# Row maxima in PSUM, a second staging tile, token subtractions on VectorE, and an order list that counts what it measured: a fused attention and two feed-forward layers

## The chip, the cores and the metric

The kernel runs on one core of a Trainium2 chip. Its engines are TensorE (PE, with its weight loads as PEld), VectorE (DVE), ScalarE (ACT), GpSimd (POOL) and SyncE (SP, which here only issues DMA transfers). The metric is the device time of one execution in microseconds. Lower is better.

## The reference

```python
scores = scale * np.matmul(q, k.transpose(0, 1, 3, 2))      # q, k, v: [4, 8, 576, 64]
log_f = np.log(np.clip(f, 0.0001, 1.0))
cum = np.cumsum(log_f, axis=-1)
decay = cum[:, :, :, None] - cum[:, :, None, :]
scores = np.where(causal, -1000000000.0, scores + decay)
scores = scores - np.max(scores, axis=-1, keepdims=True)
attn = np.exp(scores)
attn = attn / (np.sum(attn, axis=-1, keepdims=True) + 1e-09)
attn_out = np.matmul(attn, v)
...
x = attn_out.transpose(0, 2, 1, 3).reshape(2304, 512)
h = x @ w_in                                                # 512 -> 2048
x = (h * (1.0 / (1.0 + np.exp(-1.702 * h)))) @ w_out        # 2048 -> 512
g = x @ w_gate                                              # 512 -> 1536
out = (g * (1.0 / (1.0 + np.exp(-g))) * (x @ w_val)) @ w_out2
```

The weights arrive as 64-bit floats, the rest as 32-bit floats.

## The kernel before, in words

Attention handles the 32 heads in 16 pairs P. For each pair `maxima` multiplies queries with keys once (L338, and L341 for the decay), takes the maximum of each query's row on DVE (L345, with a mask that makes later keys very small), and transposes the maxima (L379). `products` multiplies again in split precision (L403), now with the maxima as a further operand, so that ACT can take the exponential straight from PSUM (L408); POOL cuts the causal edge (L412). PE then forms the values (L433) and the sums of the rows (L463). The sums travel through small transfers to a reciprocal on DVE (L478, L479) and back, and L486 divides. L338, L341 and L403 run as pairs on the upper and lower half of the array's rows, L433 as pairs on halves of its columns, L463 on quarters; the rest use the whole array.

The two layers work on token groups of 768, in two halves of 384 columns, with seven products in place of eight for each block of 2x2. `xbuild` loads a group's tokens and forms the four differences that this needs (L636, on POOL); ACT rounds them (L649) and DVE takes the remainder (L650), into the tile X. `chain` runs seven blocks of six matmuls (L673 to L675) for one unit of 256 hidden columns; ACT copies (L693) or DVE adds (L696) the blocks out of their PSUM banks. `gate`, `value` and `rounded` form the activation and split it (L757); `second` multiplies with the output weights (L777 to L779) and accumulates on DVE (L789).

`prepare` turns one unit's weights from 64 bits to 32: two loads into the tile stg, one ACT row (L556), four DVE rows (L557, L559, L561, L563), then four combinations (L579) or a split (L572), all in the tile pre, and stores to DRAM. There are 34 units; eight of them fall into attention. `stream` brings them back, rounded by L605 and L606.

What stands where on each engine is a list: each piece of work is given to `add` with its engine, a planned duration, a rank, what it reads and writes, and the PSUM banks that it takes and gives back. `order` plays the list through, each engine taking the piece of lowest rank that is ready, and so writes out one fixed order per engine. On the chip each engine works strictly through its row; semaphores hold it back where data are missing. The planned times set the order alone.

Of the kernel before, what the change touches and what calls it, by code (L numbers as in the profile page):

```python
# [31 lines left out]
LAT_PE, LAT = 330, 110  # L32
# [6 lines left out]
PSTEP, PLAG, XLEAD, PSTART = 15000, 5, 40, 205000  # L39
# [4 lines left out]
class Program:  # L44
# [12 lines left out]
    def add(self, eng, dur, rank, emit, reads=(), writes=(), lat=None, after=0, take=(), give=(), size=0):  # L57
# [16 lines left out]
        if lat is None:  # L74
            lat = LAT_PE if eng == "pe" else LAT
        self.ops.append((eng, dur, rank, emit, sorted(deps), lat, after, tuple(take), tuple(give), size))

    def order(self):
# [15 lines left out]
        moved = 0  # L94

        def at(n):
            k = len(ops[n][7])
            if not k:
                return ready_at[n]
            if len(spare) < k or held.get(ops[n][7][0][0], 0) + k > CAP:  # L100
                return 1e12
            return max(ready_at[n], spare[k - 1][0])

        while any(pools.values()):
            best = None
            for eng, pool in pools.items():
# [3 lines left out]
                n = min((n for n in pool if at(n) <= now), key=lambda n: (ops[n][2], n))  # L110
# [5 lines left out]
            o = ops[n]  # L116
            free[eng] = now + o[1]
            lat = o[5]
# [13 lines left out]
            out.append((now, n))  # L132
# [13 lines left out]
def kernel(  # L146
# [86 lines left out]
    junk = ap_.tile([128, 512], BF16, name="junk")  # L233
# [88 lines left out]
    def maxima(P):  # L322
# [21 lines left out]
        def rmax(c, t, e, o, n, end, floor=NEG):  # L344
            nc.vector.tensor_tensor_reduce(  # L345
                out=junk[:, 0:n], in0=bk("mx", P, c, e)[:, o:o + n], in1=maskw[:, end - n:end], scale=1.0,
                scalar=floor, op0=ALU.add, op1=ALU.max, accum_out=mt[i2][:, t, 32 + 64 * e:33 + 64 * e])

        def first(c, dur, *parts):
            add("pe", dur, P + RANK["max"], lambda: rmm(c, *parts), KM, take=[("mx", P, c, e) for e in range(2)])  # L350
# [5 lines left out]
        for e in range(2):  # L356
            add("dve", 720, P + RANK["maxv"], lambda e=e: rmax(0, 3, e, 0, 512, 512), MW, [("mt", i2, 3, e)], give=[("mx", P, 0, e)])
        first(1, 2 * cols(128) + 2 * cols(384), (0, 0, 0, 128), (128, 2, 0, 384))
        for e in range(2):
            add("dve", 600, P + RANK["maxv"], lambda e=e: rmax(1, 2, e, 128, 384, 512), MW + [("mx", P, 1, e)], [("mt", i2, 2, e)])  # L360
            add("dve", 320, P + RANK["maxv"], lambda e=e: rmax(1, 0, e, 0, 128, 512), MW + [("mt", i2, 2, e)], [("mt", i2, 0, e)],
                give=[("mx", P, 1, e)])
        first(2, 4 * cols(256), (0, 1, 0, 256), (256, 4, 0, 256))
        for e in range(2):
            add("dve", 400, P + RANK["maxv"], lambda e=e: nc.vector.tensor_reduce(
# [584 lines left out]
```

## Time and profile before

| | us |
|---|---|
| median of 3 runs | 1039.8 |
| lowest, highest run | 1036.37, 1040.24 |
| the profiled execution's own time | 1040.38 |
| its span, from the first to the last instruction | 1038.7 |
| PE busy | 996.5 (96%) |
| DVE busy | 788.2 (76%) |
| ACT busy | 554.2 (53%) |
| POOL busy | 219.6 (21%) |

The span is one execution. PE's busy time is that of rows whose ends are modelled, so it includes slow matmuls; what a busy PE achieves is read from how many matmuls start in a stretch.

### The profile page before, as it was taken

What the parts mean: (1) busy time and instruction counts of PE and PEld (TensorE: products, weight loads), DVE (VectorE), ACT (ScalarE), POOL (GpSimd) and SP (SyncE); (2) the same over time, 40 slices, a digit from 0 to 9 for tenths busy, and PEclk for the clock granted to TensorE, in tenths of its full rate; (3) what the DMA queues carried; (4) which work ended last, traced back from release to release, by engine and by line L of the source; (5) the groups of instructions that cost most, each with busy time, mean ns of one, the idle gap of its engine ahead of it and who ended that gap; (6) DMA issues with size and microseconds to landing.
All of it is one profiled execution on the core that took longest, in us unless ns stands there. A gap on an engine that the chain in (4) does not pass through costs nothing.

```text
span 1038.7 us, 18067 instructions
## 1 busy us (share of the span) xinstructions
PE 996.5 (96%) x6665; PEld 936.3 (90%) x6665; DVE 788.2 (76%) x1361; ACT 554.2 (53%) x947; POOL 219.6 (21%) x311
## 2 busy tenths in 40 slices
PE   6999989998899999999999899999899999999998
PEld 4766666778899999989999899999899999999998
DVE  7788779966798888988788897978855559555454
ACT  4656546665666566555654564453563556444420
POOL 3656559610422202122012200201000201000000
PEclk9999999999999999999999999999899999999999
DMA  4567778467878978978879867957655443555212
GB/s 167 188 203 225 222 261 253 140 205 230 282 232 270 322 261 303 309 287 284 297 245 315 283 227 248 325 184 269 207 166 175 157 142 115 160 163 148 95 61 102
DMA packets 118792, 226.63 MB, mean 218 GB/s; under 512 B 15120, under 2 KB 70416, under 8 KB 118704
## 3 DMA queue, kind: packets, MB, share of 16 engines
q1 hardware_dynamic: 118704, 225.48, 66.1%
q8 instruction: 52, 0.85, 0.3%
q14 instruction: 36, 0.29, 0.1%
HBM read 173.23 MB, written 52.13 MB: 217 GB/s over the span
## 4 chain that ended last, share of the span: by engine, by line
PE 79%; DVE 11%; DMA 5%; issue 2%; ACT 2%; SPq 1%; DVEq 0%; ACTq 0%
PE bank L673 10%; PE bank L674 9%; PE bank L675 9%; PE bank L778 8%; PE bank L777 8%; PE bank L779 8%; PE xx L673 3%; PE bank L403 3%; PE xx L674 3%; PE xx L675 3%; PE xx L433 3%; PE xx L778 2%; PE xx L779 2%; PE xx L777 2%; DVE junk L345 2%
## 5 line engine op out<-in xcount | busy, mean ns | idle before, releaser
L778 PE MATMUL bank<-arena,wo 128*128 128x384 f32 x458 | 154.9, 338 | 2.1 <-DVE arena L757 2.1
L777 PE MATMUL bank<-arena,wo 128*128 128x384 f32 x458 | 154.8, 338 | 0.0
L779 PE MATMUL bank<-arena,wo 128*128 128x384 f32 x458 | 154.7, 338 | 0.0
L673 PE MATMUL bank<-X,wB 128*128 128x384 f32 x340 | 114.4, 336 | 1.3 <-DVE F L696 1.2
L675 PE MATMUL bank<-X,wB 128*128 128x384 f32 x340 | 113.6, 334 | 0.0
L674 PE MATMUL bank<-X,wB 128*128 128x384 f32 x340 | 113.6, 334 | 0.0
L674 PE MATMUL bank<-X,wA 128*128 128x384 f32 x284 | 95.8, 337 | 2.8 <-DVE X L650 2.8
L673 PE MATMUL bank<-X,wA 128*128 128x384 f32 x284 | 96.2, 339 | 2.1 <-ACT X L649 2.1
L675 PE MATMUL bank<-X,wA 128*128 128x384 f32 x284 | 95.5, 336 | 0.0
L636 POOL TENSOR_TENSOR F<-F,F 128x384 f32<-128x384 f32 x13 | 16.5, 1268 | 350.6 <-DMA F<-xd 136.2
L778 PEld LDWEIGHTS bank<-arena,wo 128*128 128x128 f32 x458 | 87.3, 191 | 2.4 <-DVE arena L757 2.4
L779 PEld LDWEIGHTS bank<-arena,wo 128*128 128x128 f32 x458 | 87.4, 191 | 0.0
L777 PEld LDWEIGHTS bank<-arena,wo 128*128 128x128 f32 x458 | 87.1, 190 | 0.0
L789 DVE SCALAR_TENSOR_TENSOR arena<-bank,arena 128x384 f32<-128x384 f32 x100 | 55.3, 554 | 36.5 <-PE bank L779 36.1
L606 DVE TENSOR_TENSOR wB<-arena,wB 128x1024 fp32r<-128x1024 f32 x58 | 72.9, 1257 | 2.2 <-ACT wB L605 2.2
L345 DVE CUSTOM_DVE_ANT_0 junk<-bank,maskw 128x512 bf16<-128x512 f32 (+3 forms) x128 | 62.4, 487 | 15.7 <-PE bank L341 7.8
L403 PE MATMUL bank<-arena 64*128 64x192 f32 (+4 forms) x768 | 67.4, 317 | 5.8 <-DVE arena L345 4.5
L412 POOL TENSOR_SCALAR_AFFINE_SELECT arena<-arena 128x128 f32<-128x128 f32 (+1 forms) x160 | 55.2, 374 | 83.7 <-ACT arena L408 82.6
L403 PEld LDWEIGHTS bank<-arena 64*128 64x128 f32 x768 | 61.7, 195 | 10.9 <-DVE arena L345 6.6
L696 DVE TENSOR_TENSOR F<-F,bank 128x384 f32<-128x384 f32 x70 | 38.3, 550 | 42.4 <-PE bank L675 34.9
L636 POOL TENSOR_TENSOR arena<-arena 128x384 f32<-128x384 f32 x20 | 26.3, 1328 | 195.7 <-DMA arena<-yd 92.5
L408 ACT ACTIVATE arena<-bank 128x512 f32<-128x512 f32 (+2 forms) x128 | 55.5, 507 | 22.0 <-PE bank L403 18.4
(141 smaller groups left out, 2575.2 us busy)
## 6 DMA issues: line engine op xcount, KB each, us to landing
wo<-d_w1o SPq DMA_DIRECT2D x48, 512.0 KB
wo<-d_w2o SPq DMA_DIRECT2D x36, 512.0 KB
arena<-d_w_B SPq DMA_DIRECT2D x22, 512.0 KB
arena<-in_kq_dram SPq DMA_DIRECT2D x16, 576.0 KB
yd<-arena SPq DMA_DIRECT2D x48, 192.0 KB
arena<-d_wg_B SPq DMA_DIRECT2D x18, 512.0 KB
arena<-d_wv_B SPq DMA_DIRECT2D x18, 512.0 KB
arena<-d_w_A SPq DMA_DIRECT2D x22, 384.0 KB
```

What stands on the lines that cost most here:

```text
L345: nc.vector.tensor_tensor_reduce(out=junk[:, 0:n], in0=bk("mx", P, c, e)[:, o:o + n], in1=maskw[:, end - n:end], scale=1.0, scalar=floor, ...
L403: nc.tensor.matmul(bank[e][:, o:o + n], w[half[e]], x[half[e]], start=i == 0, stop=i == 3)
L408: nc.scalar.activation(out=ps[e][:, a:z], in_=bk("sc", P, c, e)[:, 0:z - a], func=AF.Exp, scale=0.125)
L412: nc.gpsimd.affine_select(out=q, in_=q, pattern=[[1, q.shape[1]]], compare_op=ALU.is_ge, fill=0.0, base=0, channel_multiplier=-1)
L606: add("dve", 145 + 1.04 * n, rank + 5, lambda: nc.vector.tensor_tensor(out=t[:, :, :, 1, :], in0=s, in1=f32(t[:, :, :, 0, :]), op=ALU.subt ...
L673: nc.tensor.matmul(o_, w_[:, 0, :], x_[:, 0, :], start=start and h == 0, stop=False, skip_group_check=True)
L674: nc.tensor.matmul(o_, w_[:, 0, :], x_[:, 1, :], start=False, stop=False, skip_group_check=True)
L675: nc.tensor.matmul(o_, w_[:, 1, :], x_[:, 0, :], start=False, stop=h == 1 and stop, skip_group_check=True)
L777: nc.tensor.matmul(o_, w_[:, 0, cs], gt[:, 0, :], start=q == 0, stop=False)
L778: nc.tensor.matmul(o_, w_[:, 0, cs], gt[:, 1, :], start=False, stop=False)
L779: nc.tensor.matmul(o_, w_[:, 1, cs], gt[:, 0, :], start=False, stop=q == len(tiles) - 1)
L789: add("dve", 550, r - 45, lambda x=x, a=a: nc.vector.scalar_tensor_tensor(out=a, in0=bk(*x)[:, 0:N], scalar=factor, in1=a, op0=ALU.mult, o ...
```

## The change

It has four parts. The row maximum writes its elementwise result over its own input in PSUM, and the tile junk is gone. A second tile for raw weights is laid into memory that attention has left, and preparations after the eighth alternate between the two. The four differences of `xbuild` move from POOL to DVE. And the list counts differently: per engine a latency, an overlap by which a row hands over before its end, a wait between dependent rows of one engine (100 ns on DVE), a cost for PE to change between its array modes with a small preference for keeping one, and a port that DVE and POOL can't hold together (`port`). Planned durations are replaced; two of them stand in the diff for all. Preparations are planned 13 instead of 15 us apart, from 195 instead of 205 us on.

```diff
-LAT_PE, LAT = 330, 110
+LAT = dict(pe=210, dve=112, act=135, pool=107, sp=0)
+OVER = dict(pe=0, dve=77, act=100, pool=40, sp=0)
+TURN, KEEP = 96, 0.3
+SAME = dict(pe=0, dve=100, act=0, pool=0, sp=0)
...
-PSTEP, PLAG, XLEAD, PSTART = 15000, 5, 40, 205000
+PSTEP, PLAG, XLEAD, PSTART = 13000, 5, 40, 195000
...
-        self.ops.append((eng, dur, rank, emit, sorted(deps), lat, after, tuple(take), tuple(give), size))
+            lat = LAT[eng]
+        if port is None:
+            port = eng == "pool"
+        self.ops.append((eng, dur - OVER[eng], rank, emit, sorted(deps), lat, after, tuple(take), tuple(give), size, port, mode))
...
+            if ops[n][10]:
+                return max(ready_at[n], shut[ops[n][0]])
...
-                n = min((n for n in pool if at(n) <= now), key=lambda n: (ops[n][2], n))
+                n = min((n for n in pool if at(n) <= now),
+                        key=lambda n: (ops[n][2] - (KEEP if eng == "pe" and ops[n][11][0] == shape[-1] else 0), n))
...
+            if eng == "pe":
+                if o[11][0] != shape[-1]:
+                    now += TURN
+                shape = o[11]
+            if o[10]:
+                shut["pool" if eng == "dve" else "dve"] = now + o[1] + OVER[eng]
...
-                ready_at[u] = max(ready_at[u], now + o[1] + (0 if same else lat))
+                ready_at[u] = max(ready_at[u], now + o[1] + (SAME[eng] if same else lat))
...
-    junk = ap_.tile([128, 512], BF16, name="junk")
...
         def rmax(c, t, e, o, n, end, floor=NEG):
+            b_ = bk("mx", P, c, e)[:, o:o + n]
             nc.vector.tensor_tensor_reduce(
-                out=junk[:, 0:n], in0=bk("mx", P, c, e)[:, o:o + n], in1=maskw[:, end - n:end], scale=1.0,
+                out=b_, in0=b_, in1=maskw[:, end - n:end], scale=1.0,
...
-            add("dve", 720, P + RANK["maxv"], lambda e=e: rmax(0, 3, e, 0, 512, 512), MW, [("mt", i2, 3, e)], give=[("mx", P, 0, e)])
+            add("dve", 692, P + RANK["maxv"], lambda e=e: rmax(0, 3, e, 0, 512, 512), MW, [("mt", i2, 3, e)], give=[("mx", P, 0, e)])
...
+    stgs = [stg, put("stg", 1, 2048).bitcast(U32).rearrange("p (h c b) -> p h c b", h=2, b=2)]
...
-        src, st, p = SRC[kind][u], stg, pre
+        src, st, p = SRC[kind][u], stgs[s_], pre
...
-        G, P_ = ["stg"], ["pre"]
+        G, P_ = [("stg", s_)], ["pre"]
...
-                add("pool", 1060, rank - 8, lambda: nc.gpsimd.tensor_tensor(
-                    out=F[o_], in0=F[a_], in1=F[b_], op=ALU.subtract), [FS[a_], FS[b_]] + FK, [FS[o_]])
+                add("dve", 550, rank - 8, lambda: nc.vector.tensor_tensor(
+                    out=F[o_], in0=F[a_], in1=F[b_], op=ALU.subtract), [FS[a_], FS[b_]] + FK, [FS[o_]], port=True)
...
-        prepare(*it, rk(PSTEP * n) + PLAG, PSTART + PSTEP * n)
+        prepare(*it, rk(PSTEP * n) + PLAG, PSTART + PSTEP * n, n % 2)
```

In the changed file the lines stand further down: L345 becomes L361, L557 to L563 become L576 to L582, L579 becomes L598, L606 L625, L636 L655, L650 L669, L696 L715, L757 L776 and L789 L808.

DVE in one pair of attention, before: the row maxima of the two heads, each followed by a row that reads its result out (shown once). bank_88 to bank_93 are PSUM banks, arena_61 holds the maxima.

```order
L345 ISA junk,arena_61<-bank_91,maskw 128x512 [waits PE_49]
L345 ISA arena_61 128x1
L345 ISA junk,arena_61<-bank_89,maskw 128x512 [waits DVE_49,PE_49]
...
L345 ISA junk,arena_61<-bank_92,maskw 128x384 [waits DVE_49,PE_49]
...
L345 ISA junk,arena_61<-bank_92,maskw 128x128 [waits DVE_49]
...
L345 ISA junk,arena_61<-bank_90,maskw 128x384 [waits DVE_49,PE_49]
```

And DVE at that place of the changed kernel:

```order
L361 ISA bank_90,arena_61<-bank_90,maskw 128x512 [waits PE_49]
L361 ISA arena_61 128x1
L361 ISA bank_88,arena_61<-bank_88,maskw 128x512 [waits PE_49]
...
L361 ISA bank_89,arena_61<-bank_89,maskw 128x384 [waits PE_49]
...
L361 ISA bank_87,arena_61<-bank_87,maskw 128x384 [waits PE_49]
...
L361 ISA bank_89,arena_61<-bank_89,maskw 128x128 [waits DVE_49]
```

The waits on DVE's own semaphore are gone from the larger rows, and the two 384-column rows stand ahead of the two of 128 columns on the same banks.

DVE in the first layer, before, at the 20th preparation: pre is its tile, stg the raw weights, F the staged tokens and results, arena_62 among others the sums of L789.

```order
L557 TENSOR_SCALAR pre<-pre 128x2x512
L559 TENSOR_SCALAR pre<-pre 128x2x512
L561 SCALAR_TENSOR_TENSOR pre<-stg,pre 128x2x512
L563 SCALAR_TENSOR_TENSOR pre<-stg,pre 128x2x512
L579 TENSOR_TENSOR pre<-pre 128x2x128 x4
L696 TENSOR_TENSOR F_76<-F_76,bank_88 128x384
L789 SCALAR_TENSOR_TENSOR arena_62<-bank_93,arena_62 128x384
```

And DVE of the changed kernel at the same preparation:

```order
L715 TENSOR_TENSOR F_76<-F_76,bank_92 128x384
L576 TENSOR_SCALAR pre<-pre 128x2x512
L715 TENSOR_TENSOR F_75<-F_75,xx 128x384
L578 TENSOR_SCALAR pre<-pre 128x2x512
L669 TENSOR_TENSOR X<-F_74,X 128x384
L580 SCALAR_TENSOR_TENSOR pre<-arena_62,pre 128x2x512
L808 SCALAR_TENSOR_TENSOR arena_62<-bank_89,arena_62 128x384
L582 SCALAR_TENSOR_TENSOR pre<-arena_62,pre 128x2x512
L808 SCALAR_TENSOR_TENSOR arena_62<-bank_91,arena_62 128x384
L598 TENSOR_TENSOR pre<-pre 128x2x128
```

The eight rows of the preparation stood one behind the other; now another row stands between any two of them, often one that reads a PSUM bank (L715, L808). The raw weights come from the second tile, in arena_62.

POOL before, from the last mask of attention on: its subtractions for two half groups of tokens and the start of a third.

```order
L412 AFFINE_SELECT arena_62<-arena_62 128x128 x2
L636 TENSOR_TENSOR F_74<-F_74,F_73 128x384
L636 TENSOR_TENSOR F_73<-F_74 128x384 x2
L636 TENSOR_TENSOR F_74<-F_73 128x384
L636 TENSOR_TENSOR arena_62<-arena_62 128x384 x4
```

DVE of the changed kernel, with the subtractions of one half group a little behind the preparation above:

```order
L655 TENSOR_TENSOR F_74<-F_74,F_73 128x384
L655 TENSOR_TENSOR F_73<-F_74 128x384 x2
L655 TENSOR_TENSOR F_74<-F_73 128x384
L715 TENSOR_TENSOR F_76<-F_76,bank_91 128x384
L625 TENSOR_TENSOR wA_64<-arena_62,wA_64 128x6x128
L808 SCALAR_TENSOR_TENSOR arena_62<-bank_89,arena_62 128x384
```

POOL had nothing else to do at that time. On DVE the four stand ahead of rows that free banks and round weights.

## Rows read from the trace of the kernel before

**Rows 1.** Stretches: length, busy time of each engine (instructions), PEclk, DMA.

```profile
20.00:227.60 207.60, 196.63 (x2136) 144.83 (x2135) 169.04 (x447) 123.28 (x245) 119.68 (x224) 0.98 0.65 203
227.60:1034.90 807.30, 790.08 (x4489) 784.59 (x4488) 605.28 (x875) 422.26 (x695) 91.11 (x64) 0.99 0.67 223
760.00:1034.90 274.90, 274.90 (x1588) 274.79 (x1586) 160.54 (x229) 118.64 (x198) 11.59 (x8) 1.00 0.43 133
```

**Rows 2.** The same view, one short stretch in the first layer.

```profile
468.00:471.40 3.40, 3.40 (x12) 3.40 (x11) 3.01 (x6) 2.96 (x6) 0.00 (x0) 0.50 0.84 320
```

**Rows 3.** PE's timeline in attention: start, duration, line, tiles, form, count.

```profile
78.09 0.75 PE L379 MATMUL bank<-arena 128*128 128x128 f32 x5
...
80.11 3.68 PE L403 MATMUL bank<-arena 64*128 64x384 f32 x48
...
87.06 0.28 PE L338 MATMUL bank<-arena 64*128 64x256 f32 x2
87.18 0.28 PE L341 MATMUL bank<-arena 64*128 64x256 f32 x2
87.39 1.51 PE L433 MATMUL xx<-arena 128*64 128x448 f32 x8
...
90.66 0.50 PE L338 MATMUL bank<-arena 64*128 64x512 f32 x2
```

**Rows 4.** PE's waits from 20 to 227.6: us in total, times, longest.

```profile
PE bank L403 <- DVE arena L345: 4.5, 8, 0.8
...
PE bank L338 <- DVE arena L345: 1.3, 2, 1.2
```

**Rows 5.** PE's timeline in the layers, rows behind idle time (in brackets, with its end's cause).

```profile
273.35 0.63 PE L673 MATMUL bank<-X,wA 128*128 128x384 f32 x1 [2.06 <-ACT X L649]
...
466.45 0.44 PE L674 MATMUL bank<-X,wA 128*128 128x384 f32 x1 [2.33 <-DVE X L650]
...
596.96 0.44 PE L777 MATMUL xx<-arena,wo 128*128 128x384 f32 x1 [1.69 <-DVE arena L789]
```

**Rows 6.** DVE's timeline: one preparation beside POOL, and one without it.

```profile
456.69 0.69 DVE L557 TENSOR_SCALAR pre<-pre 128x1024 f32<-128x1024 f32 x1 [0.47 <-DMA arena<-yd]
...
462.75 2.25 DVE L579 TENSOR_TENSOR pre<-pre 128x256 f32<-128x256 f32 x4
...
465.85 0.55 DVE L650 TENSOR_TENSOR X<-F,X 128x384 fp32r<-128x384 f32 x1
...
646.27 0.69 DVE L557 TENSOR_SCALAR pre<-pre 128x1024 f32<-128x1024 f32 x1
...
650.24 1.56 DVE L579 TENSOR_TENSOR pre<-pre 128x256 f32<-128x256 f32 x4
```

**Rows 7.** POOL's timeline in the same time as the first of these.

```profile
457.10 1.15 POOL L636 TENSOR_TENSOR F<-F,F 128x384 f32<-128x384 f32 x1 [32.33 <-DMA F<-xd]
458.33 5.26 POOL L636 TENSOR_TENSOR F<-F 128x384 f32<-128x384 f32 x3
```

**Rows 8.** DVE's timeline in attention: row maxima with and without a wait.

```profile
64.88 0.41 DVE L345 CUSTOM_DVE_ANT_0 junk<-bank,maskw 128x256 bf16<-128x256 f32 x1
...
65.22 0.42 DVE L365 TENSOR_REDUCE arena<-bank 128x1 f32<-128x256 f32 x1
...
68.06 0.69 DVE L345 CUSTOM_DVE_ANT_0 junk<-bank,maskw 128x512 bf16<-128x512 f32 x1 [0.61 <-PE bank L341]
...
68.90 0.69 DVE L345 CUSTOM_DVE_ANT_0 junk<-bank,maskw 128x512 bf16<-128x512 f32 x1
```

**Rows 9.** Lines 292 and 284: duration in ns (shortest, median, longest), starts, form.

```profile
L292 DVE MEMSET xx<- x1: 378/378/378, 4.8 to 4.8; 128x384 f32 x1
...
L284 DVE MEMSET arena<- x2: 592/592/592, 1.6 to 3.6; 128x640 f32 x2
```

**Rows 10.** Timeline of SP's issues and of POOL around one token load.

```profile
706.70 2.30 SPq L254 DMA_DIRECT2D F<-yd  x3
...
712.92 1.02 POOL L636 TENSOR_TENSOR F<-F,F 128x384 f32<-128x384 f32 x1 [39.26 <-DMA F<-yd]
```

More of the change, by code (lines that the diff above doesn't have):

```diff
@@ L55, in __init__, with add @@
         self.later = {}
-    def add(self, eng, dur, rank, emit, reads=(), writes=(), lat=None, after=0, take=(), give=(), size=0):
+    def add(self, eng, dur, rank, emit, reads=(), writes=(), lat=None, after=0, take=(), give=(), size=0, port=None, mode="FF"):
         n = len(self.ops)
@@ L94, in order @@
         moved = 0
+        shut, shape = dict(dve=0, pool=0), "FF"
         def at(n):
             k = len(ops[n][7])
+            if ops[n][10]:
+                return max(ready_at[n], shut[ops[n][0]])
             if not k:
@@ L116, in order @@
             o = ops[n]
+            lat = o[5]
+            start = now
+            if eng == "pe":
[4 more added lines that the diff above has]
+                shut["pool" if eng == "dve" else "dve"] = now + o[1] + OVER[eng]
             free[eng] = now + o[1]
-            lat = o[5]
             if o[9]:
@@ L131, in order @@
             spare.sort()
-            out.append((now, n))
+            out.append((start, n))
             for u in users[n]:
                 same = ops[u][0] == eng and eng != "sp"
-                ready_at[u] = max(ready_at[u], now + o[1] + (0 if same else lat))
+                ready_at[u] = max(ready_at[u], now + o[1] + (SAME[eng] if same else lat))
                 left[u] -= 1
@@ L344, in rmax @@
         def rmax(c, t, e, o, n, end, floor=NEG):
+            b_ = bk("mx", P, c, e)[:, o:o + n]
             nc.vector.tensor_tensor_reduce(
-                out=junk[:, 0:n], in0=bk("mx", P, c, e)[:, o:o + n], in1=maskw[:, end - n:end], scale=1.0,
+                out=b_, in0=b_, in1=maskw[:, end - n:end], scale=1.0,
                 scalar=floor, op0=ALU.add, op1=ALU.max, accum_out=mt[i2][:, t, 32 + 64 * e:33 + 64 * e])
         def first(c, dur, *parts):
-            add("pe", dur, P + RANK["max"], lambda: rmm(c, *parts), KM, take=[("mx", P, c, e) for e in range(2)])
+            add("pe", dur, P + RANK["max"], lambda: rmm(c, *parts), KM, take=[("mx", P, c, e) for e in range(2)], mode="SS")
         DK = [("dk", P % 2, c) for c in range(2)]
@@ L380, in turn @@
                                  start=True, stop=True)
-        add("pe", 800, P + RANK["turn"], turn, [("mt", i2, t, e) for t in range(5) for e in range(2)] + ["identr"],
+        add("pe", 570, P + RANK["turn"], turn, [("mt", i2, t, e) for t in range(5) for e in range(2)] + ["identr"],
             take=[("turn", P, c) for c in range(2)])
@@ L464, in sums @@
                                              start=k == 0, stop=k == len(lst) - 1)
-        add("pe", c4(128, *[S - QH] * 3, 192, 64), P + RANK["sum"], sums, kp(0, 1, 2, 3) + ["ones32"], ["xb0"])
+        add("pe", 1850, P + RANK["sum"], sums, kp(0, 1, 2, 3) + ["ones32"], ["xb0"], mode="VW")
         add("act", 650, P + RANK["ev"], lambda: nc.scalar.copy(out=xs[ix], in_=xx[:, 384:960]), ["xb0", "xb1"], [("xs", ix), "evd"])
@@ L543, in ring_of, with prepare @@
         return i % n
-    def prepare(kind, u, rank, after=0):
-        src, st, p = SRC[kind][u], stg, pre
+    def prepare(kind, u, rank, after=0, s_=0):
+        src, st, p = SRC[kind][u], stgs[s_], pre
         flat = st.rearrange("p h c b -> p (h c b)")
@@ L567, in prepare @@
                 sp(rank, cv[:, h], src[h], (), P_, 3500, after)
[L568 removed]
+        G = [("stg", s_), ("stg1", s_)]
         if kind.endswith("o"):
@@ L740, in value @@
         add("dve", 1350, rk(pos[4]) - 50, lambda: nc.vector.tensor_tensor(
-            out=F[:, 0:3, :], in0=F[:, 0:3, :], in1=V, op=ALU.mult), VK + FK, FS[0:3])
+            out=F[:, 0:3, :], in0=F[:, 0:3, :], in1=V, op=ALU.mult), VK + FK, FS[0:3], port=True)
     def rounded(lay, g, u, t):
```

57 lines of the change are left out of this document (28 added, 29 removed).

## The prediction

> **What bounds the kernel now.** I read the stretches first, since attention and the two feed-forward layers have different limits [rows 1]. From 227.6 us, when the last attention product is done, to 1034.9 us only the layers' matmuls run. In the last 274.9 us PE never stops: 1588 matmuls, so one costs 0.1731 us. At that pace the 4488 matmuls of the layers' stretch need 776.9 us of its 807.3: 30.4 us are lost. 17.2 of them are idle (807.3 - 790.1). The mean granted clock of 0.99 stands for another 8.1 (1% of 807.3), which are stretches at the lower of the two levels, 1.2 of 2.4 GHz; the one shown lies right behind a stop of PE [rows 2]. The remaining 5 are restarts.
>
> For attention the pace comes from a stretch without a stop [rows 3]. From 80.11 to 90.66 PE does one head pair's products except the transposes, 10.55 us, and these take 0.75: 11.3 us, 180.8 for 16 pairs. About a third of a pair lies before 20 us (3.6), and 48 matmuls of the layers inside (8.3). So the 207.6 us up to 227.6 hold 185.5 of work and 22.1 of loss. In total 52 us can be won, and no edit makes a matmul faster.
>
> Who holds PE up? In attention mostly DVE's row maxima, which free the PSUM banks: 5.8 us of idle PE in ten waits [rows 4]. In the layers it is DVE at one remove. The stalls of 2.06, 2.33 and 1.69 us [rows 5] each end behind a run of weight-preparation rows on DVE. One of them: from 456.69 to 465.00 eight such rows in a row, while POOL runs its four subtractions for the next token group (457.10 to 463.59) [rows 6, 7]. The bank-freeing L696, L789 and the rounding L650 stand behind the run. Elsewhere, with POOL quiet, the same eight rows take 646.27 to 651.80 [rows 6], 5.53 us and not 8.31.
>
> **The change, part by part.**
>
> *Row maxima into PSUM.* The result of an L345 goes onto its own input instead of into the one tile junk. By the two lists, 138 of the 160 rows wait for an earlier row of DVE itself before, and 85 afterwards. Two 512-column rows with that wait start 0.84 us apart, although one lasts 0.69; a 256-column row of 0.41 without it lets the next start after 0.34 [rows 8]. So a row can be followed after its duration less 0.07, and the wait costs 0.84 - 0.62 = 0.22. 53 of them are 11.7 us of DVE, in a stretch where PE waits ten times for exactly these rows. No row shows a DVE operation of this kind that writes PSUM. The nearest are two memsets: 378 ns for 384 columns into PSUM, 592 for 640 into SBUF [rows 9]; per column 0.98 and 0.93. Lower bound of the extra cost 0, upper the 6% between these two, 0.03 us for a mean row and 5 us over 160. I take 0, because the shorter row carries the larger share of whatever is fixed.
>
> *Order list.* The list now counts 100 ns between two dependent rows of DVE, where it counted 0, and picks another ready row for the gap. The order excerpts on the preparation show it: its run is cut up, and a bank-freeing row stands after nearly every one of its rows. The longest a freed bank can wait behind preparation falls from 5.5 to 8.3 us (the run) to about 1.2 to 1.9 (one row). This is the largest term. It takes the three shown stalls, 6.1 us idle, and two of them were followed by a half-clock stretch (at 273.35 the first matmul already lasts 0.63), which costs half of the 3.4 us shown, 1.7 each: 9.5. Of the other 11.1 us of idle time I count half as of the same kind, 5.5. Together 15 of the 30.4.
>
> What stays: the hand-over at 247 us, where DVE's L486 waits for the chain of small transfers that brings the sums back (the rows between the reciprocal and that product are about as many as before), and the burst of X roundings at 743, which has no preparation in it.
>
> *Attention's list* gets measured latencies and the knowledge that POOL and DVE hold each other up. With the 0.22s gone I let it take back the ten waits for DVE but one, 5.2, their restarts at an estimated 0.25 each, 2.5, and half of what the clock lost there (mean 0.98 [rows 1], 4.2), 2.1: 10 of 22.1. Against this, PE changes between its row-paired, column-paired and full-array products 135 times up to the last sum, where it did 123 times. Two row-paired products follow each other after 0.12, a column-paired one after 0.21 [rows 3]: 0.09 for a change, 1.1 us. Also 36 matmuls that ran inside attention now run behind it: neutral, since they must run somewhere.
>
> *Subtractions from POOL to DVE.* 72, four for each of 18 half groups. On DVE one costs at most 0.55, the price of an L650 of the same shape [rows 6]: 2.2 us for four. What DVE gets back is the stretching, 8.31 - 5.53 = 2.8 in the burst shown, if it has such rows throughout, and nothing if it is idle. DVE is busy 605 of 807 us [rows 1], 75%: 2.1. So the move costs DVE between 18 x 2.2 = 40 and -11 us, and by that share 2, which I count as nothing for PE: a row of 0.5 us between bank-freeing rows is less than the rows of preparation already there. The cover is DVE's idle quarter; without it the 2 us would be PE's. The Trainium skill ("SBUF — State Buffer", section "Who interferes with whom") says that a VectorE row with two SBUF inputs and a GpSimd row that reads SBUF exclude each other for a whole instruction. By that rule four subtractions, 1.02 us each where nothing is in their way [rows 10], would take 4.1 us from DVE in such a run, not 2.8, and the move would give back some 15 us of DVE work; the trace shows the stretching, but less of it.
>
> *Second staging tile, earlier and denser preparation.* The loads of every other preparation no longer wait for the one before. No PE wait names these loads. The first eight preparations, all that fall into attention, still use one tile, and the result tile pre is still single. The last preparation stands behind 76 of DVE's 128 L789 before and 78 after, so the nominal pace of 13 us instead of 15 changes nothing. Worth 0; the cover is that preparation runs far ahead of the streams.
>
> Sum, against the profiled execution's 1040.4 (0.6 above the median of the runs): -10 + 1 - 15 = -24, so 1016.
>
> **Rivals.**
>
> *Half of it.* The layers' first 120 us lose POOL's help when DVE has most to do, and the list's gaps are filled with rows that are themselves late, so new stalls of the old size come. For it: 16 subtractions fall there. Against: the cut-up runs. Attention alone gives 1040 - 10 + 1 = 1031; with a part of the rest 1028.
>
> *Nothing moves.* PE's stalls are the list's own errors on transfers, which this change doesn't measure anew; other stalls take their place. 1036 to 1043.
>
> *Slower: DVE waits for tokens.* On POOL a subtraction could wait for its tokens for free. On DVE the wait blocks all behind it, the bank-freeing rows above all. The last of four token loads of one half group is issued by about 709.0, and POOL starts on it at 712.92 [rows 10], some 4 us later. If the list expects them earlier than they land, each of the 16 half groups in the layers costs the error. From 24/16 = 1.5 us each it eats the gain; at 3 us the time is 1016 + 48 = 1064. Against it: the changed list puts more work between load and subtraction than the old one did.
>
> *More.* If the hand-over and the burst at 743 go too, another 10: 1006.
>
> **Chances.** Forecast 0.58, own range 1007 to 1024; more 0.08; half 0.18; nothing 0.08; slower 0.08. What a measurement of this kernel can tell from no change is about 0.5%, 5 us: below 1034.6 is faster. Forecast, more and half: 0.84 faster, 0.08 the same, 0.08 slower. The range of 1001 to 1034 leaves out the last two cases and little of the first.
>
> **What would show it.** Row maxima of 512 columns start 0.62 to 0.70 apart with durations unchanged at 0.69; a longer duration would show the price of PSUM. L579 takes 0.42 throughout in the layers, its four rows apart, and POOL is silent after attention. The last L463 ends at 210 to 217 us. PE idle behind preparation (L674 for X, L777 for a bank) is gone, the layers' stretch loses some 15 us instead of 30. The prediction is wrong if DVE's subtractions show idle time in front of them that ends with a DMA, or if the sum of PE's idle time in the layers is still 17 us.

## The result, and the profile after

The changed kernel takes 1027.0 us (median of 4 runs, 1022.17 to 1029.58) where the one before takes 1039.4: ratio 0.988, interval 0.9838 to 0.9922. In a second comparison of five rounds the ratio was 0.990 (0.9872 to 0.9928). The forecast was 1016, range 1001 to 1034: the sign and the range hold, but the gain is about half, outside the forecast's own range (1007 to 1024) and where the rival "half of it" (1028) put the time. The profiled execution is the shortest of its four, 1022.17 (span 1020.4), so the trace shows 18 us of gain where the medians show 12; a second profile, below, shows 10.

The two stretches of the trace after (columns as in [rows 1]), and the first 29 us of the layers:

```profile
20.00:212.60 192.60, 185.42 (x2090) 133.74 (x2086) 142.68 (x432) 113.81 (x231) 105.04 (x216) 0.98 0.65 202
212.60:242.00 29.40, 24.28 (x135) 22.47 (x132) 22.70 (x37) 19.41 (x29) 0.00 (x0) 1.00 0.71 221
...
212.60:1016.70 804.10, 790.93 (x4528) 783.34 (x4524) 605.82 (x957) 429.82 (x705) 0.00 (x0) 1.00 0.69 228
```

Attention ends at 212.6 instead of 227.6. By the working of the prediction it holds 179.3 us of work now (185.5 less 36 matmuls that moved behind it), so 13.3 are lost instead of 22.1. The layers need 4524 x 0.1731 = 783.1 of their 804.1: 21.0 lost instead of 30.4. The forecast had -9 and -15; this trace has -8.8 and -9.4. DVE's busy time in the layers is what it was, 605.8 against 605.3, with 64 subtractions more on it and POOL silent. Of the layers' 21 us, 6.0 fall into the first 29: 29.4 less 135 matmuls.

PE's waits: the one of attention that ends with row maxima (compare [rows 4]), then the two longest of the layers; us in total, times, longest.

```profile
PE bank L395 <- DVE arena L361: 1.9, 3, 1.0
...
PE bank L692 <- ACT F L712: 3.5, 3, 1.9
PE bank L694 <- DVE wA L625: 1.9, 3, 1.3
```

Row maxima hold PE for 1.9 us instead of 5.8. In the layers the stops behind L650 (now L669) and L789 (now L808), named in [rows 5], are all but gone; what leads the list now are evictions by ACT (L712) and rounded weights (L625). Most of these lie where attention hands over to the layers. PE's timeline there, the rows behind idle time, the first with its neighbours:

```profile
213.60 0.34 PE L694 MATMUL bank<-X,wB 128*128 128x384 f32 x1
214.50 0.45 PE L692 MATMUL bank<-X,wB 128*128 128x384 f32 x1 [0.57 <-ACT F L712]
214.79 0.34 PE L693 MATMUL bank<-X,wB 128*128 128x384 f32 x1
...
219.54 0.44 PE L694 MATMUL bank<-X,wA 128*128 128x384 f32 x1 [1.29 <-DVE wA L625]
225.68 0.44 PE L692 MATMUL bank<-X,wA 128*128 128x384 f32 x1 [1.01 <-ACT F L712]
237.14 0.44 PE L694 MATMUL bank<-X,wA 128*128 128x384 f32 x1 [0.32 <-DVE wA L625]
241.10 0.45 PE L692 MATMUL bank<-X,wA 128*128 128x384 f32 x1 [1.93 <-ACT F L712]
```

And ACT and DVE in that time:

```profile
222.48 1.28 ACT L743 ACT_TABLE_LOAD   x1
223.78 1.49 ACT L743 ACTIVATE F<-F 128x1536 f32<-128x1536 f32 x1
225.17 0.46 ACT L712 COPY F<-bank 128x384 f32<-128x384 f32 x1
```

```profile
211.09 0.76 DVE L502 TENSOR_TENSOR arena<-arena 128x576 f32<-128x576 f32 x1 [4.19 <-DMA arena<-rw]
...
218.20 0.42 DVE L598 TENSOR_TENSOR pre<-pre 128x256 f32<-128x256 f32 x1
218.54 0.95 DVE L625 TENSOR_TENSOR wA<-arena,wA 128x768 fp32r<-128x768 f32 x1
```

Before, the same place had two stops, 3.0 us, of which the prediction let the one of 2.06 stay; a stretch at a granted clock of 0.50 came right behind it:

```profile
239.19 0.44 PE L673 MATMUL bank<-X,wB 128*128 128x384 f32 x1 [0.98 <-DVE F L696]
249.02 0.44 PE L778 MATMUL bank<-arena,wo 128*128 128x384 f32 x1 [2.06 <-DVE arena L757]
```

```profile
227.60:257.00 29.40, 26.36 (x141) 25.69 (x141) 20.34 (x34) 17.76 (x30) 0.00 (x0) 0.94 0.73 234
249.60:252.90 3.30, 3.30 (x12) 3.30 (x11) 3.27 (x8) 2.50 (x4) 0.00 (x0) 0.50 0.39 149
```

So five stops, 5.1 us, stand where two of 3.0 stood, but the first 29.4 us of the layers lost 5.0 before (29.4 less 141 matmuls) and lose 6.0 now: the hand-over is worse by 1 us only. Now DVE stands 4.19 us before L502, which waits for the sums on their way back (L486 before); preparation and evictions pile up behind it, and L625 comes at 218.54 for a matmul due at 218.1. On ACT the long activation L743 and its table load stand in front of the eviction L712, and once more L743 alone before 241.10. Attention ended 15 us earlier; the table load starts at 222.5 where it started at 222.9. The other 8.0 of the 13.2 us of idle PE lie behind 242 us in stops of at most 1.2, most of them at evictions and at L776, the split of the activation.

### The profile page after: what moved, and what is told of

Read it like the earlier page. It is cut to its first block, busy times and chain, and to the rows that moved or that the text cites. A ratio compares the mean times of both kernels' runs of the same rounds, so it can differ in the third digit from the quotient of the medians.

```text
span 1020.4 us, 18032 instructions
## 1 busy us (share of the span) xinstructions
PE 985.3 (97%) x6665; PEld 923.9 (91%) x6665; DVE 763.5 (75%) x1433; ACT 552.4 (54%) x947; POOL 113.9 (11%) x239
## 4 chain that ended last, share of the span: by engine, by line
PE 85%; DVE 6%; DMA 4%; issue 2%; ACT 1%; SPq 1%; POOL 0%; DVEq 0%; POOLq 0%; ACTq 0%
PE bank L694 9%; PE bank L692 9%; PE bank L693 9%; PE bank L797 8%; PE bank L798 8%; PE bank L796 8%; PE bank L419 5%; PE xx L449 4%; PE xx L692 4%; PE xx L694 4%; PE xx L693 4%; PE xx L796 2%; PE xx L798 2%; PE xx L797 2%; PE xx L479 2%
## 5 line engine op out<-in xcount | busy, mean ns | idle before, releaser
L797 PE MATMUL bank<-arena,wo 128*128 128x384 f32 x442 | 147.8, 334 | 1.5 <-DVE arena L776 1.5
L796 PE MATMUL bank<-arena,wo 128*128 128x384 f32 x442 | 147.8, 334 | 1.2 <-ACT arena L773 1.2
L798 PE MATMUL bank<-arena,wo 128*128 128x384 f32 x442 | 147.7, 334 | 0.0
L692 PE MATMUL bank<-X,wB 128*128 128x384 f32 x360 | 120.5, 335 | 0.6 <-ACT F L712 0.6
L694 PE MATMUL bank<-X,wB 128*128 128x384 f32 x360 | 120.4, 334 | 0.1
L693 PE MATMUL bank<-X,wB 128*128 128x384 f32 x360 | 120.3, 334 | 0.0
L715 DVE TENSOR_TENSOR arena<-arena,bank 128x384 f32<-128x384 f32 x85 | 46.8, 551 | 59.3 <-ACT arena L712 33.4
L692 PE MATMUL bank<-X,wA 128*128 128x384 f32 x254 | 85.4, 336 | 2.9 <-ACT F L712 2.9
L694 PE MATMUL bank<-X,wA 128*128 128x384 f32 x254 | 85.2, 336 | 1.9 <-DVE wA L625 1.9
L693 PE MATMUL bank<-X,wA 128*128 128x384 f32 x254 | 84.9, 334 | 0.0
L797 PEld LDWEIGHTS bank<-arena,wo 128*128 128x128 f32 x442 | 83.0, 188 | 2.0 <-DVE arena L776 2.0
L796 PEld LDWEIGHTS bank<-arena,wo 128*128 128x128 f32 x442 | 83.0, 188 | 1.5 <-ACT arena L773 1.5
L798 PEld LDWEIGHTS bank<-arena,wo 128*128 128x128 f32 x442 | 83.0, 188 | 0.0
L808 DVE SCALAR_TENSOR_TENSOR arena<-bank,arena 128x384 f32<-128x384 f32 x102 | 56.5, 554 | 32.8 <-PE bank L798 32.4
L361 DVE CUSTOM_DVE_ANT_0 bank<-bank,maskw 128x512 f32<-128x512 f32 (+3 forms) x128 | 59.1, 520 | 26.1 <-PE bank L356 26.1
L625 DVE TENSOR_TENSOR wB<-arena,wB 128x1024 fp32r<-128x1024 f32 x58 | 70.7, 1219 | 8.9 <-ACT wB L624 8.9
L419 PEld LDWEIGHTS bank<-arena 64*128 64x128 f32 x768 | 58.6, 194 | 13.3 <-issue 8.5
L692 PEld LDWEIGHTS bank<-X,wB 128*128 128x128 f32 x360 | 67.6, 188 | 1.1 <-ACT F L712 0.9
L694 PEld LDWEIGHTS bank<-X,wB 128*128 128x128 f32 x360 | 67.6, 188 | 0.4 <-DVE wB L625 0.4
L428 POOL TENSOR_SCALAR_AFFINE_SELECT arena<-arena 128x128 f32<-128x128 f32 (+1 forms) x160 | 58.5, 394 | 81.7 <-ACT arena L424 80.7
L693 PEld LDWEIGHTS bank<-X,wB 128*128 128x128 f32 x360 | 67.6, 188 | 0.0
```

Source lines behind the costliest of these rows:

```text
L361: nc.vector.tensor_tensor_reduce(out=b_, in0=b_, in1=maskw[:, end - n:end], scale=1.0, scalar=floor, op0=ALU.add, op1=ALU.max, accum_out=m ...
L419: nc.tensor.matmul(bank[e][:, o:o + n], w[half[e]], x[half[e]], start=i == 0, stop=i == 3)
L428: nc.gpsimd.affine_select(out=q, in_=q, pattern=[[1, q.shape[1]]], compare_op=ALU.is_ge, fill=0.0, base=0, channel_multiplier=-1)
L625: add("dve", 145 + 1.04 * n, rank + 5, lambda: nc.vector.tensor_tensor(out=t[:, :, :, 1, :], in0=s, in1=f32(t[:, :, :, 0, :]), op=ALU.subt ...
L692: nc.tensor.matmul(o_, w_[:, 0, :], x_[:, 0, :], start=start and h == 0, stop=False, skip_group_check=True)
L693: nc.tensor.matmul(o_, w_[:, 0, :], x_[:, 1, :], start=False, stop=False, skip_group_check=True)
```

## The experiments

Each ran in five rounds beside the kernel before, whose median was 1035.9, 1037.1 and 1037.7 in the three sets, so ratios compare best. First what they gave together. The three columns on the right are from one profiled execution each; the two of the changed kernel differ by 5.0 in loss, so smaller differences there say little. "Loss" is the length of the stretch behind attention less its number of matmuls (4487 to 4529, by their own records, so up to 0.4 off the numbers above) times 0.1731; "weights" is PE's idle time there that ends with L624, L625 (L605, L606 before) or a load of weights.

```
kernel                                       median  ratio (interval)          layers' loss  idle PE  weights
before                                       1039.4                            30.8          17.2      0
changed                                      1027.0  0.988  (0.9838-0.9922)    21.2          13.2      2.5
changed, again                               1028.0  0.990  (0.9872-0.9928)    26.2          15.0      2.2
 maxima into junk again                      1027.9  0.9913 (0.9887-0.9939)    22.8          13.2      1.7
 no gap between DVE's dependent rows         1034.1  0.9979 (0.9960-0.9998)    29.5          19.1      6.3
 one staging tile, old pace                  1048.1  1.0092 (1.0063-1.0122)    43.1          30.3     20.6
 subtractions on POOL                        1056.4  1.0192 (1.0163-1.0220)    58.2          41.7     20.7
 the same, port off for them                 1059.3  1.0211 (1.0180-1.0242)    54.4          33.1     11.9
 the same, new dates                         1037.6  1.0000 (0.9980-1.0020)    30.4          17.4      0
 new dates alone (subtractions on DVE)       1020.0  0.9814 (0.9788-0.9839)    15.2           8.6      2.3
before with the new counting alone           1083.7  1.0446 (1.0417-1.0476)    80.8          57.2     34.6
before with maxima into PSUM                 1033.1  0.9961 (0.9938-0.9983)    26.3          17.9      0
before with subtractions on DVE              1061.5  1.0227 (1.0195-1.0259)    50.6          29.3      7.2
 the same, DVE's rows counted 77 ns shorter  1034.9  0.9969 (0.9947-0.9991)    17.0          10.0      0.6
```

**First set: undo one part of the change.** The changed kernel once more:

> The changed kernel once more, so that the others stand against it on one chip, and for a second profile. Both theories: 1022 to 1030 us, ratio 0.983 to 0.992. If the half-clock stretches are what sets its runs apart, the idle time of PE is the same as in the first profile (5.5 us in attention from 20 us on, some 13 us after it), and the difference of the two spans is in stretches at a granted clock of 0.5.

Measured 1028.0; the profiled execution took 1030.45. Idle time in attention is the same (7.4 against 7.2), in the layers 1.8 more, and the layers have two stretches of 3.4 us at a granted clock of 0.50, where the first profile has none there. Each costs half its length, 1.7; with the idle time that is 5.2, and the layers' loss differs by 5.0. The other 3.4 of the 8.3 us between the two profiles are in attention, and I leave them open. The expectation was right in part: one stop that lasted 0.02 us in the first profile lasts 2.13 here. Behind it the clock falls, and also behind the stop of 1.94, which stood in the first profile too (241.10, 1.93) and was followed there by a clock of 1.00.

```profile
244.19 0.45 PE L692 MATMUL bank<-X,wA 128*128 128x384 f32 x1 [1.94 <-ACT F L712]
...
661.64 0.69 PE L692 MATMUL xx<-X,wB 128*128 128x384 f32 x1 [2.13 <-DVE F L715]
```

```profile
245.10:248.40 3.30, 3.30 (x12) 3.30 (x11) 2.28 (x5) 2.97 (x5) 0.00 (x0) 0.50 1.06 254
661.50:664.80 3.30, 3.16 (x10) 3.16 (x11) 3.16 (x7) 0.49 (x1) 0.00 (x0) 0.50 1.00 345
```

Row maxima back into SBUF:

```diff
-                out=b_, in0=b_, in1=maskw[...]
+                out=junk[:, 0:n], in0=b_, in1=maskw[...]
```

> The changed kernel with one thing undone: the row maxima write their elementwise result into the tile junk in SBUF again; list, order and durations of the list unchanged. Theory of the prediction (the waits between row maxima cost PE its banks in attention): 64-odd waits of 0.22 us come back, 512-column rows start 0.84 apart again, the last product of sums ends some 8 us later and the time is 1035. Rival (the gain in attention is the new order's, and DVE has enough slack there): within 3 us of the changed kernel, 1025 to 1030, with longer DVE and no more idle PE.

Measured 1027.9, the rival's. The waits are back, 512-column rows start 0.85 apart, and DVE is busy for 149.9 us from 20 us to the end of attention instead of 142.7; attention ends at 213.3 all the same.

```profile
63.33 0.69 DVE L362 CUSTOM_DVE_ANT_0 junk<-bank,maskw 128x512 bf16<-128x512 f32 x1 [0.47 <-PE bank L357]
64.18 0.69 DVE L362 CUSTOM_DVE_ANT_0 junk<-bank,maskw 128x512 bf16<-128x512 f32 x1
```

No gap between dependent rows:

```diff
-SAME = dict(pe=0, dve=100, act=0, pool=0, sp=0)
+SAME = dict(pe=0, dve=0, act=0, pool=0, sp=0)
```

> The changed kernel, with the list counting 0 instead of 100 ns between dependent rows of DVE. Theory of the prediction (the cut-up preparation is the largest term in the layers): preparation stands in runs of eight again, PE's idle time behind them returns, +9 to +15 us, 1036 to 1042. Rival (it is POOL's silence: a run without POOL lasts 5.5 and not 8.3 us and hides behind free banks): at most 2 us more, 1025 to 1031.

Measured 1034.1, 6 us over the changed kernel of the same set and between the two. The gap is worth 6, not 15. Preparation does stand in runs of eight again, twelve of them. But the stops that return are not the old ones for tokens and banks: the largest new item is rounded weights (L625), 6.3 us.

Subtractions on POOL:

```diff
-                add("dve", 550, rank - 8, lambda: nc.vector.tensor_tensor(
+                add("pool", 1060, rank - 8, lambda: nc.gpsimd.tensor_tensor(
```

> The changed kernel with the 72 subtractions on POOL again, everything else as changed (the list recounts). Theory of the prediction (the move is worth nothing by itself): within 4 us of the changed kernel, 1023 to 1031. Rival (POOL's silence is the gain in the layers): DVE's rows are stretched again beside POOL, some 8 to 10 us of the layers' gain go, 1035 to 1037.

Measured 1056.4: slower than before, and far outside both. Half of PE's idle time ends with weights, the longest stop lasts 13.0 us. Neither theory had this.

**Second set: one part alone, and the port.** 

```diff
-                    out=F[o_], in0=F[a_], in1=F[b_], op=ALU.subtract), [FS[a_], FS[b_]] + FK, [FS[o_]])
+                    out=F[o_], in0=F[a_], in1=F[b_], op=ALU.subtract), [FS[a_], FS[b_]] + FK, [FS[o_]], port=False)
```

> The changed kernel with the subtractions on POOL, and the list told that these 72 rows leave DVE alone (port off for them; the other rows keep it). In the run with the subtractions on POOL and port on, the preparation stood later in DVE's list (the 18th behind 103 evictions instead of 92) and PE stopped for up to 13 us for weights. Theory A (the list's port accounting pushes the preparation back until weights are late): the 18th preparation stands behind 96 evictions again, the stops for weights go, 1027 to 1036. Theory B (the stretching of DVE's rows beside POOL is itself the cost): 1048 or more, as with port on.

Measured 1059.3. Theory A falls as an account of the time: the preparation stands earlier in the order, and the kernel is no faster. The number is theory B's. In the two profiles weights cost 11.9 instead of 20.7 and idle PE falls by as much, but the loss falls by 3.8 only, and the median not at all.

The new counting alone (junk, POOL, one tile and old pace put back into the changed file):

> The kernel before with the new counting of the list alone: junk, one staging tile with its old pace, and the subtractions on POOL as before. Theory of the prediction (the list is the largest term): 1020 to 1030. Theory A (counting the port while POOL has the subtractions delays preparation): slower than before, 1045 to 1060, with PE stopped for weights. Theory B says the same as the prediction at most, since the stretching is that of before: 1026 to 1036.

Measured 1083.7, the slowest of all and outside every range. So what I called the largest term of the gain costs 46 us by itself. Its attention is as short as that of the changed kernel, though, with junk and all: it ends at 213.4. PE's longest wait behind it is for rounded weights (its lines stand one further down, L624 is L625):

```profile
PE bank L693 <- ACT wA L625: 26.9, 3, 19.4
```

Row maxima into PSUM alone, in the order of before:

> The kernel before with the row maxima's elementwise results in PSUM, nothing else; the order is that of before. Theory of the prediction (the waits between row maxima hold the banks): the ten stops of PE behind row maxima, 5.8 us, and their restarts go, 1028 to 1032 where before has 1036. Rival, as far as the run with junk back in the changed kernel bears it out (DVE has slack for the 0.22 us there): within 3 us of before.

Measured 1033.1, 0.9961: 4 us gained, between the two. In the old order the waits cost something, in the new one nothing.

Subtractions on DVE alone:

> The kernel before with the subtractions on DVE, nothing else; the old counting of the list. Prediction: worth nothing by itself, within 4 us of before (1032 to 1040). Theory B (the stretching beside POOL is the cost): preparation in runs of eight stays but lasts 5.5 us, the stops behind it shrink from 2.1 to 2.3 us to under 1, and 8 us are gained, 1028. Rival with DVE blocked on token loads: idle DVE that ends with a DMA of tokens, slower than before.

Measured 1061.5, outside all three. No stop ends with a transfer of tokens; PE waits behind bunches of DVE's rows, at the longest for L696 (4.3 us) and for L757 (3.7).

Two parts that each cost 24 and 46 us alone save 12 together with the rest. After this set I took the parts for conditions of one another, and looked for what each of them needs.

**Third set: what the parts need.** One staging tile and the old pace:

```diff
-        prepare(*it, rk(PSTEP * n) + PLAG, PSTART + PSTEP * n, n % 2)
+        prepare(*it, rk(PSTEP * n) + PLAG, PSTART + PSTEP * n, 0)
```

> The changed kernel with one staging tile for all preparations and the old pace (15 us apart from 205 us on). Prediction (second tile and pace are worth 0, preparation runs far ahead): within 4 us of the changed kernel, 1023 to 1031. Theory C (the cut-up preparations take longer from load to store, and the last of them meet the first token group of the second layer; there the tile decides): PE stops for weights between 690 and 740 us as in the runs with POOL, 15 to 25 us more, 1040 to 1052.

Measured 1048.1, theory C. The longest wait of PE, and the preparations on ACT and the transfers on SP ahead of it:

```profile
PE xx L692 <- ACT wA L624: 12.6, 1, 12.6
```

```profile
699.27 1.14 ACT L575 ACTIVATE pre<-stg 128x1024 f32<-128x1024 f32 x1 [1.84 <-DMA stg<-in_wg_dram]
...
716.95 0.83 ACT L624 CAST wA<-arena 128x768 fp32r<-128x768 f32 x1 [0.72 <-DMA arena<-d_wg_A]
```

```profile
690.42 1.21 SPq L269 DMA_DIRECT2D d_w2o<-stg  x2
...
693.98 0.89 SPq L269 DMA_DIRECT2D stg<-in_wg_dram  x2
...
710.19 0.52 SPq L269 DMA_DIRECT2D d_wg_A<-pre  x1
...
713.65 0.33 SPq L269 DMA_DIRECT2D arena<-d_wg_A  x1
```

The load of the next raw weights (693.98) stands behind the stores of the last result, the first of which (690.42) reads the same tile; then ACT, eight rows of DVE between other rows, the store at 710.19, the load back at 713.65, the rounding at 716.95, and PE goes on at 717.8. The same steps in the changed kernel: the raw weights of that preparation go into the second tile (arena) while the one before still works in the first, and its result is stored at 683.11, 27 us earlier.

```profile
650.79 0.81 SPq L269 DMA_DIRECT2D arena<-in_wg_dram  x2
...
670.38 1.21 SPq L269 DMA_DIRECT2D d_w2o<-stg  x2
...
683.11 0.52 SPq L269 DMA_DIRECT2D d_wg_A<-pre  x1
```

Preparation does not run far ahead: in the second layer's first group it meets its use. This run takes back the tile and the pace together, so how the 20 us divide between them is not shown.

Subtractions on POOL, port off for them, and new dates in the list. They are a set for which the list itself plans no stop near 700 us:

```diff
-SAME = dict(pe=0, dve=100, act=0, pool=0, sp=0)
+SAME = dict(pe=0, dve=110, act=0, pool=0, sp=0)
...
-LEAD = 30
+LEAD = 60
...
-PSTEP, PLAG, XLEAD, PSTART = 13000, 5, 40, 195000
+PSTEP, PLAG, XLEAD, PSTART = 9000, -10, 30, 195000
```

> The subtractions on POOL with the list told that they leave DVE alone (1059 us in the last run of that kind), and only the list's dates moved: preparation 9 instead of 13 us apart and ranked 15 earlier, tokens 10 later, weights fetched 30 earlier, 110 instead of 100 ns between dependent rows. Theory C (POOL's price was the late weights, which dates can mend): the stops for weights between 700 and 745 us go and the time is 1028 to 1038. Theory B (the stretching of DVE's rows beside POOL is the price): 1050 or more still.

Measured 1037.6: 22 us come back and no stop for weights is left, theory C. B is out as the whole price. And the same dates with the subtractions on DVE:

> The changed kernel, subtractions on DVE, with the same new dates as the kernel with POOL in this set. Theory C: the remaining stops for weights around 720 us (2.6 us in the first profile) go, 1018 to 1026. If dates matter little once weights are early: 1024 to 1030. The stops between 213 and 242 us, which wait for small transfers and evictions on ACT, should stay in either case.

Measured 1020.0, ratio 0.9814: theory C, and faster than both kernels. The stops at the hand-over stay (218 to 247 us, six of 4.5 in all), as expected. Between the two kernels lie 17.5 us; they differ in the engine of the 72 rows and in the order that the list makes of it, which no run holds apart. DVE in the kernel with POOL, part of one preparation, then POOL, then one of PE's two longest waits behind attention:

```profile
283.11 0.55 DVE L715 TENSOR_TENSOR F<-F,bank 128x384 f32<-128x384 f32 x1 [0.48 <-PE bank L694]
...
285.35 1.39 DVE L578 TENSOR_SCALAR pre<-pre 128x1024 uint32<-128x1024 uint32 x1
286.66 1.36 DVE L669 TENSOR_TENSOR X<-arena,X 128x384 fp32r<-128x384 f32 x1
287.94 2.03 DVE L580 SCALAR_TENSOR_TENSOR pre<-arena,pre 128x1024 uint32<-128x1024 uint32 x1
```

```profile
282.56 5.05 POOL L655 TENSOR_TENSOR arena<-arena 128x384 f32<-128x384 f32 x4 [16.89 <-DMA arena<-xd]
287.57 1.33 POOL L655 TENSOR_TENSOR F<-F,F 128x384 f32<-128x384 f32 x1
```

```profile
PE bank L693 <- DVE X L669: 5.4, 6, 1.9
```

An L669 lasts 1.36 beside POOL instead of 0.55, an L580 2.03 instead of 1.22, and PE waits for just these token roundings. In the layers DVE is busy 608.9 us without the subtractions and 605.7 with them: moving them away from it saves it nothing.

These rows take turns. The L669 ends at 288.02, 0.41 behind the POOL row that ends at 287.61; the next POOL row ends at 288.90, 0.88 behind that L669; the L580 ends at 289.97, 1.07 behind that POOL row. Each of these is what the row takes alone (0.55, 1.02, 1.22) less about 0.14, so a long row is a short one whose record holds its wait. All 16 rows of L669 that run into a POOL row end 0.41 to 0.42 behind it. A row with one input in PSUM doesn't wait: the L715 at 283.11 takes its 0.55 while POOL is at work. The Trainium skill ("SBUF — State Buffer", section "Who interferes with whom") lets VectorE rows with two SBUF inputs and GpSimd rows that read SBUF exclude each other for a whole instruction; the trace agrees.

The kernel before, subtractions on DVE, one number of the new list:

```diff
-        self.ops.append((eng, dur, rank, emit, ...
+        self.ops.append((eng, dur - (77 if eng == "dve" else 0), rank, emit, ...
```

> The kernel before with the subtractions on DVE (1061 us by itself) and one number of the new list: every row of DVE is counted 77 ns shorter, which is the overlap by which a row hands over. No gap between dependent rows, junk and the one staging tile as before. Theory D (the list with the old durations takes DVE for full and pushes its evictions and preparations to the last moment; the overlap alone mends that): the stops between 435 and 570 us go and the time is 1028 to 1036. The prediction's view (the gap of 100 ns, which cuts preparation up, is the largest term): the runs of eight stay, no gain over before, 1038 or more.

Measured 1034.9, theory D: 26.6 us come back by one number, and the layers' loss is 17.0, less than in the changed kernel, with preparation in runs, one tile and junk. As a whole it is only 3 us faster than before; its attention, where the list's other numbers are the old ones, ends at 228.7.

## Why the prediction was half right

**What held.** The sign, attention's size in the first trace (-8.8, in the second -5.3, forecast -9), DVE's busy time (forecast +2, measured +0.5), and neither sign of being wrong came: PE's idle time in the layers is 13.2 and 15.0 us, not 17. The mark for preparation came too, here a run of it after the change, no row of it longer than alone:

```profile
471.55 1.23 DVE L580 SCALAR_TENSOR_TENSOR pre<-stg,pre 128x1024 uint32<-128x1024 uint32 x1
...
475.97 0.42 DVE L598 TENSOR_TENSOR pre<-pre 128x256 f32<-128x256 f32 x1
```

Eight rows that took 5.5 alone and 8.3 beside POOL [rows 6] lie spread over 7.9 us, from 470.10 to 477.99: cut up, a preparation is done later than in an undisturbed run. The rival of DVE blocked by token loads is out: no subtraction has idle time before it. The view of L655 (shortest, median, longest ns) has none to name:

```profile
L655 DVE TENSOR_TENSOR F<-F x39: 547/551/645, 165.7 to 845.1; 128x384 f32<-128x384 f32 x39
...
its engine sat idle before it (us, times) until:
who waited for it (us, times):
```

**Step "order list takes 15 of the layers' 30.4".** The loss fell by 9.6 in the first profile and 4.6 in the second. The three shown stalls, 6.1, went. Of the other 11.1 us of idle time half was to go; 13.2 stand there now, 15.0 in the second profile, since new stops of up to 2.1 us came, at the hand-over and behind it. And the larger part of the first profile's gain is not idle time: idle went from 17.2 to 13.2, the loss beyond it from 13.6 to 8.0. The clock is in that; its mean in this stretch rose from 0.99 to 1.00. (The restart that attention's sum put at an estimated 0.25 can be read at 214.50: that matmul and the next come 0.84 late by the pace of 0.1731, with 0.57 idle, so 0.27.)

**Step "second staging tile: worth 0, preparation runs far ahead".** It failed most: without the tile and the new pace the changed kernel takes 20 us more. I had counted how many evictions stand before the last preparation, and not when PE wants what it prepares.

**Step "subtractions: nothing for PE".** DVE's sum came out right and the conclusion wrong. What counts is how long the tokens' chain and each row beside it take, not DVE's sum: 17.5 us with dates that fit POOL, 28 with the ones of the change. But on DVE they cost 24 us in the old list. The prediction also read the 2.8 us of [rows 6, 7] as less than exclusion would cost, since it put 1.02 on each of POOL's four rows. But the four DVE rows of that burst that run into them (three are shown, the fourth is the first L579) last only 0.69 to 0.71 longer than alone (0.69, 1.22, 1.22, 0.42), 2.8 together, since at each turn about 0.14 of DVE's row and of POOL's lies beside the other. What it called stretching is the exclusion itself.

```profile
457.41 1.39 DVE L559 TENSOR_SCALAR pre<-pre 128x1024 uint32<-128x1024 uint32 x1
458.83 1.92 DVE L561 SCALAR_TENSOR_TENSOR pre<-stg,pre 128x1024 uint32<-128x1024 uint32 x1
460.79 1.93 DVE L563 SCALAR_TENSOR_TENSOR pre<-stg,pre 128x1024 uint32<-128x1024 uint32 x1
```

**Step "order list: the gap of 100 ns is the largest term, 15".** It is worth 6. In the old list the overlap of 77 ns gives 26.6 us once the subtractions are on DVE; I take it that a list which books DVE's rows at full length takes the engine for full, and that the same holds in the new list, where no run takes the overlap away. And the counting helps only with the rest: alone it costs 46 us, 34.6 of idle PE for weights.

**Step "with the 0.22s gone".** The waits were sized right (starts 0.85 apart with them), and they cost 4 us in the old order and nothing in the new one. Attention's gain is the new order's: the run with the new counting alone has it too.

**What is luck.** That the time still fell into the range does not speak for the sum: two terms put at nothing are worth 17 to 28 us in the new order, and the largest one 6 where it stood at 15. By the ratios below, these two mostly make good what the new counting costs without them, which the sum did not count either.

That the change as a whole gains 12 and that the counting alone and the subtractions alone lose 46 and 24 is shown by the runs. By the ratios, the changed kernel without the tile and pace is 1.9% slower, and without the subtractions on DVE 2.9%; the counting alone, which lacks both and the PSUM part, is 5.5% slower than the changed kernel, so the two together are nearly as large as its loss. The orders show the way: the 18th preparation starts on DVE behind 17 rows of L789 before and 20 of L808 after, behind 23 with one tile or port off, 26 with the subtractions on POOL, and 28 with the counting alone, and these four are the kernels that stop longest for weights. Which number of the new counting pushes it back is open; port off was tried only in the kernel with two tiles.

## What to carry to other kernels

A part of a change that "is worth 0 because something runs ahead" needs the time at which its product is used, read at the tightest place, not the position of its last row. Before parts are added up, ask which of them only make room for the others: here the cut-up order needs the second tile with the new pace, and the subtractions need the list's shorter rows. An engine's busy sum says little when the loss is in a chain: DVE's in the layers was 605.3, 605.8 and 605.7 us in three kernels (before, changed, new dates) of which the first and last are 18 us apart.

## What the hardware showed that I had not expected

A row maximum that writes PSUM costs a little more. Before, then after (ns: shortest, median, longest):

```profile
L345 DVE CUSTOM_DVE_ANT_0 junk<-bank,maskw x128: 291/480/692, 12.0 to 211.5; 128x512 bf16<-128x512 f32 x32, 128x384 bf16<-128x384 f32 x32, 128x128 bf16<-128x128 f32 x32, 128x256 bf16<-128x256 f32 x32
```

```profile
L361 DVE CUSTOM_DVE_ANT_0 bank<-bank,maskw x128: 324/510/733, 12.0 to 197.8; 128x512 f32<-128x512 f32 x32, 128x384 f32<-128x384 f32 x32, 128x128 f32<-128x128 f32 x32, 128x256 f32<-128x256 f32 x32
```

By form the medians grow by 39 ns at 128 columns, 26 at 256, 40 at 384 and 8 at 512; the 320-column rows, which start from a maximum, by 2 (551, then 553). In the mean of the 160 rows it is 27 ns. It is no fixed amount: with the maxima in PSUM in the old order the medians grow by 8, 18, 40, 33 and 4. The row that reads the maximum out goes from 83 to 141 in the median, and lies wholly beside the next row:

```profile
63.10 0.70 DVE L361 CUSTOM_DVE_ANT_0 bank<-bank,maskw 128x512 f32<-128x512 f32 x1 [0.66 <-PE bank L356]
63.71 0.14 DVE L361 DVE_READ_ACCUMULATOR2_ANT arena<- 128x1 fp32r x1
63.71 0.73 DVE L361 CUSTOM_DVE_ANT_0 bank<-bank,maskw 128x512 f32<-128x512 f32 x1
```

So two 512-column rows start 0.61 apart, as forecast. The price lies just under the upper bound of 0.03 us that I had set and not taken, and shows in no time here: with junk back the kernel takes as long.

And idle time of PE costs more than itself: in the layers the loss beyond the idle time is 6.6 us where 8.6 are idle (new dates), 13.6 where 17.2 are (before) and 23.6 where 57.2 are (new counting alone). The mean granted clock of these stretches is 1.00, 0.99 and 0.97. The kernel before with maxima into PSUM has as much idle time as before, 17.9, and loses 8.4 beyond it, at a mean clock of 1.00: with equal idle time the difference goes with the clock.
